# Attention with relative bias and a feed-forward layer on one core: a one-element memset ahead of the last four loads of v

## The chip, the core and the metric

The kernel runs on one core of a Trainium2 chip. The metric is the device time of one execution in microseconds (us). The engines in the profile are PE (TensorE, matmuls; PEld is its weight loads), DVE (VectorE), ACT (ScalarE), POOL (GpSimd) and SP (SyncE, which here only issues DMAs). DMAs that GpSimd issues are in the queue that the profile calls software_dynamic, those of SyncE in hardware_dynamic; both use the core's 16 DMA engines.

## The reference

Attention over 8 batches, 8 heads, 576 positions and a head width of 64, with a bias that depends on the distance of two positions, and behind it a feed-forward layer over all 8 x 576 = 4608 tokens:

```python
scores = scale * q @ k.transpose(0, 1, 3, 2) + bias      # bias from a table of 32 buckets per head
attn = softmax(scores)
x = (attn @ v).transpose(0, 2, 1, 3).reshape(B * S, H * D)   # 4608 x 512
h = x @ w_in                                              # 512 -> 2048
out = np.maximum(0.01 * h, h) @ w_out                     # 2048 -> 512
```

## The kernel before

Work goes by pairs of heads: pair n = 4 b + p is heads 2p and 2p + 1 of batch b, 32 pairs in all. For one pair:

- VectorE copies q and k of the pair, 96 rows wide, from the batch's tiles qn and kn into one of three buffers pr (`rows`, L440). From pair 9 on a DMA of SyncE turns them into a tile tu (`turn_by_dma`, L445; called "the turn" below), and VectorE or ScalarE copies that to qt and kt (L471, L475).
- PE makes the scores (L497 to L505), ScalarE takes the exponential (L511 to L518), VectorE multiplies with the bias (L531), and PE multiplies with v (`av`, L552 and L567), where a column of ones gives the sum.
- VectorE divides by that sum into one of three tiles opair (`norm`, L579, L580), and a DMA of SyncE transposes opair into xT[p], which holds the tokens of four batches in a ring (`x_dma`, L586; pairs 7 and 31 and the first ones go through PE instead). The names that end in numbers, xT_78 to xT_81, are xT[0] to xT[3].

The feed-forward layer goes by tiles T of 512 tokens. The tile T = 2 begins with the last pair of batch 2 (pair 11), T = 3 with that of batch 3 (pair 15), T = 4 with pair 19, T = 5 with pair 23: PE multiplies with w_in (L619; L676 for the last tiles, with fewer products after the sums of L653), ScalarE applies the leaky maximum (L695), PE multiplies with w_out (L749), and VectorE combines the products in y (L760, L765), whose blocks SyncE stores (L769). Seven products stand for eight, so y's blocks are reused, and a write to one waits for the store of the tile before.

The loads of q, k and v are DMAs of GpSimd, which cast float32 to bfloat16. v of batch b goes into vn[b % 2] and v4[b % 2], six DMAs (L307, L313), and can start when PE has read v of batch b - 2 there. The tiles of q and k are double too (L299, four DMAs for a batch).

All engines run in the order in which the program is written, which a planner sets ahead of time: `Plan` places tasks by estimated costs, due times and a table of shifts. `pool_load` puts the loads into one line on GpSimd; in it stand, for each batch b from 2 on, q and k of b, and then v of b. The planner's list of what the load of v waits for has held, for b > 3, the output transpose of the last pair of batch b - 2 (the `xt` of `plan_loads`), but the list only sets the order and the planned times: the program itself waits only for semaphores of data that an instruction reads or writes.

Of the kernel before, what the change touches and what calls it, by code (L numbers as in the profile page):

```python
# [79 lines left out]
class Plan:  # L80
# [37 lines left out]
    def add(self, engine, cost, after, go, rank, take=(), give=(), tail=0.0, at=None):  # L118
        t = {"engine": engine, "cost": cost, "after": list(after), "go": go, "rank": rank, "n": len(self.tasks),
             "take": list(take), "give": list(give), "tail": tail, "end": at, "start": at}  # L120
        if at is None:
            self.tasks.append(t)
        return t
# [95 lines left out]
def kernel(  # L219
# [10 lines left out]
    nc = tc.nc  # L230

    B, H, S, D = q.shape
# [5 lines left out]
    n_pairs = H // 2  # L238
# [24 lines left out]
    RING = 4  # L263
    RT = RING * S
    xT = [per.tile([P, RT + P - SL], BF16, name=f"xT{p}") for p in range(n_pairs)]
# [29 lines left out]
    def load_qk(b, h0, h1, js=(0, 1)):  # L295
        i = b % NBUF
        for j in js:
            src, dst = ((q, qn[i]), (k, kn[i]))[j]
            nc.gpsimd.dma_start(  # L299
                out=dst[0:RQ, h0:h1, :, :].rearrange("r h c d -> r h (c d)"),  # L300
                in_=src[b, h0:h1, :, :].rearrange("h (r c) d -> r h (c d)", c=NC),
            )

    def load_v_part(b, j):
        i = b % NBUF
        for c in ((0,), (1, 2), (3,))[j]:
            nc.gpsimd.dma_start(  # L307
                out=vn[i][:, c, :, 0:D],
                in_=v[b, :, c * P : (c + 1) * P, :].rearrange("h s d -> s h d"),
            )  # L310
        if j == 2:
            for e in range(2):
                nc.gpsimd.dma_start(  # L313
                    out=v4[i][e * SL : (e + 1) * SL, :, e, 0:D],
                    in_=v[b, e::2, NJ * P : S, :].rearrange("h s d -> s h d"),
                )

    def clear_v(eng, i):
        eng.memset(v4[i], 0.0)
        for e in range(2):  # L320
            eng.memset(v4[i][e * SL : (e + 1) * SL, :, e, D : D + 1], 1.0)
        eng.memset(vn[i][:, :, :, D : D + 1], 1.0)
# [452 lines left out]
    rowt, cut, sct, ext, avt, nrt, nmt, xt, vt = {}, {}, {}, {}, {}, {}, {}, {}, {}  # L775
# [19 lines left out]
    def moves(t, work, lane, lead, least, yields=0.39):  # L795
        t["moves"], t["lane"], t["lead"], t["least"], t["yields"] = work, lane, lead, least, yields
        return t

    def pool_load(key, cost, go, work, after=(), rank=1):
        t = add("POOL", cost, prev + list(after), go, rank)  # L800
        moves(t, work, 0, min(cost + 1.0, 3.2), cost + 2.2, 0.39 if key[0] in ("qk", "v") else 0.2)
        prev[:] = [t]
        L[key] = t
        return t
# [5 lines left out]
    prev.append(clears[0])  # L810
    pool_load(("qk", 0, 2), 1.4, lambda: load_qk(0, 6, H), 2.0, rank=-9)
    pool_load(("v", 0), 5.2, lambda: [load_v_part(0, j) for j in range(3)], 5.5, rank=-8)
    vt[0] = L["v", 0]
    edges = add("POOL", 1.0, list(prev), lambda: [clear_edges(nc.gpsimd, i) for i in range(3)], -7)
    pool_load(("qk", 1, 0), 1.4, lambda: load_qk(1, 0, 4), 2.6, rank=-4)
    pool_load(("w_in", 0), 0.8, lambda: load_w_in(0), WH, rank=-4)
    clears.append(add("POOL", 1.2, list(prev), lambda: clear_v(nc.gpsimd, 1), -3))
    prev.append(clears[1])
    vt[1] = pool_load(("v", 1), 5.2, lambda: [load_v_part(1, j) for j in range(3)], VB, rank=-2)
    pool_load(("qk", 1, 1), 1.4, lambda: load_qk(1, 4, H), 2.7, rank=-1)  # L820
    pool_load(("w_in", 1), 0.8, lambda: load_w_in(1), WH, rank=6)
# [139 lines left out]
    def plan_loads(b):  # L961
        i = n_pairs * (b - 2)
        for hh in range(2):
            ps = [rowt[i + 2 * hh + x][r] for x in range(2) for r in range(2)]
            pool_load(("qk", b, hh), 1.5, lambda hh=hh: load_qk(b, 4 * hh, 4 * hh + 4), 3.0, ps, 10 * i + 500)
        avs = [t for p in range(n_pairs) for t in avt[i + p]]
        if b > 3:
            avs = avs + xt[i + n_pairs - 1]
        vt[b] = pool_load(("v", b), 5.0, lambda: [load_v_part(b, j) for j in range(3)], 5.0, avs, 10 * i + 500)

    oin, ins = {}, {}

# [110 lines left out]
    for n in range(N):  # L1083
        if n >= 2 * n_pairs and n % n_pairs == 0:
            plan_loads(n // n_pairs)
        plan_rows(n)
        if n == 0:
            plan_table()
            clears[1]["after"].append(hk4t[1])
        plan_pair(n)  # L1090
# [47 lines left out]
```

## Time and profile before

| | us |
|---|---|
| median of 3 runs (lowest, highest) | 364.35 (362.64, 365.35) |
| the profiled execution | 364.15 |
| its span, from the first to the last instruction | 362.3 |

The granted clock is 1.000 throughout. The page gives PE as busy for 97% of the span, VectorE 81%, ScalarE 76%, GpSimd 19%. Attention runs to about 262 us, beside the feed-forward tiles that are ready by then; from there on only feed-forward products are left. A row of the timeline gives the start, the length, the engine, the line, the operation and, in brackets, how long the engine stood idle before it and what ended that. A row of the DMA view gives what is moved, how many DMAs began or were being issued in the window, their size and the median time from issue to landing.

### The profile page before, as it was taken

The numbers are of one execution on the slowest core, as the hardware profiler recorded it, in microseconds if no ns is written. First come the engines' busy times: TensorE is split into PE (matmuls) and PEld (weight loads), VectorE is DVE, ScalarE is ACT, GpSimd is POOL, SyncE is SP. The second block draws the span as 40 slices with busy tenths as digits, with TensorE's granted clock in tenths as the row PEclk, the third lists the DMA queues.
The fourth block names the chain that finished last, engine by engine and source line by source line (L and its number), as shares of the span: only waits on it lengthen the run. The fifth ranks groups of instructions, "written<-read, shape, count | busy, mean of one in ns | idle before, by whom it ended". The sixth has DMA issues, their size and how long they took to land.

```text
span 362.3 us, 10124 instructions
## 1 busy us (share of the span) xinstructions
PE 351.4 (97%) x4206; PEld 256.6 (71%) x4206; DVE 292.4 (81%) x703; ACT 275.8 (76%) x365; POOL 70.2 (19%) x107
## 2 busy tenths in 40 slices
PE   8999999999999899999998999999999999999996
PEld 6665457745677365654676777667888888888885
DVE  6978799885799559957679979999986778686594
ACT  6987998689778799799988897897737546756520
POOL 8955132080006200800350050000000000000000
PEclk9999999999999999999999999999999999999999
DMA  8999999999539993997499799312120020020022
GB/s 126 151 187 196 208 184 146 132 140 194 130 81 101 202 155 58 133 170 87 59 172 173 103 148 116 97 34 52 51 76 2 31 88 31 2 87 31 31 87 89
DMA packets 106941, 39.31 MB, mean 108 GB/s; under 512 B 82320, under 2 KB 105872, under 8 KB 106896
## 3 DMA queue, kind: packets, MB, share of 16 engines
q0 software_dynamic: 53424, 18.21, 50.0%
q1 hardware_dynamic: 53120, 20.03, 31.6%
q8 instruction: 33, 0.54, 0.6%
q10 hardware_dynamic: 352, 0.43, 0.4%
q14 instruction: 12, 0.10, 0.1%
HBM read 36.70 MB, written 9.44 MB: 127 GB/s over the span
## 4 chain that ended last, share of the span: by engine, by line
PE 52%; DMA 5%; DVE 5%; ACT 5%; issue 2%; DVEq 0%; ACTq 0%
PE pm L749 20%; PE pm L676 12%; PE pm L619 9%; PE ps_s L497 4%; DMA xT<-opair 3%; PE ps_o L567 2%; PE ps_om L567 2%; ACT at L511 2%; DMA out_dram<-y 2%; ACT gt L695 2%; DVE sum L717 1%; DVE y L765 1%; PE ps_s L501 1%; PE ps_s L504 1%; DVE opair L580 1%
## 5 line engine op out<-in xcount | busy, mean ns | idle before, releaser
L511 ACT ACTIVATE at<-ps_s 128x1024 bf16<-128x1024 f32 x124 | 121.3, 1041 | 19.6 <-PE ps_s L497 17.1
L619 PE MATMUL pm<-xT,w_in_sb 128*128 128x512 bf16 (+1 forms) x416 | 86.4, 346 | 3.7 <-DMA xT<-opair 1.6
L531 DVE TENSOR_TENSOR at<-at,hk 128x768 bf16<-128x768 bf16 (+4 forms) x156 | 66.5, 449 | 18.1 <-ACT at L511 14.0
L619 PEld LDWEIGHTS <-w_in_sb 128*128 128x128 bf16 x416 | 37.6, 98 | 35.5 <-issue 9.2
L749 PEld LDWEIGHTS <-gt 128*128 128x128 bf16 x576 | 54.2, 98 | 11.8 <-issue 3.4
L695 ACT ACTIVATE gt<-pm 128x512 bf16<-128x512 f32 x88 | 51.0, 643 | 12.7 <-PE pm L619 12.4
L307 POOL DMA_DIRECT2D vn<-in_v_dram x32 | 28.9, 915 | 133.2 <-PE ps_o L567 70.8
L765 DVE TENSOR_TENSOR y<-pm,y 128x512 f32<-128x512 f32 (+1 forms) x53 | 41.0, 774 | 13.5 <-PE pm L749 13.2
L749 PEld LDWEIGHTS <-sum 128*128 128x128 bf16 x432 | 40.9, 98 | 7.9 <-issue 2.1
L567 PEld LDWEIGHTS <-at 128*128 128x128 bf16 x1240 | 41.6, 98 | 3.4 <-issue 0.9
L497 PE MATMUL ps_s<-qt,kt 64*128 64x512 bf16 x256 | 39.9, 381 | 0.6 <-ACT at L513 0.3
L749 PE MATMUL pm<-w_out_sb,gt 128*128 128x256 bf16 x288 | 37.1, 273 | 0.0
L749 PE MATMUL pm<-mix,gt 128*128 128x256 bf16 x288 | 36.6, 273 | 0.0
L749 PE MATMUL pm<-w_out_sb,sum 128*128 128x256 bf16 x288 | 35.7, 273 | 0.0
L567 PE MATMUL ps_o<-vn,at 128*128 128x65 bf16 x640 | 25.5, 193 | 0.6 <-DMA vn<-in_v_dram 0.5
L680 ACT COPY at<-pm 128x1024 f32<-128x1024 f32 x15 | 15.1, 1008 | 12.5 <-PE pm L676 12.5
L686 DVE TENSOR_TENSOR at<-pm,at 128x512 f32<-128x512 f32 (+1 forms) x22 | 19.0, 879 | 6.8 <-ACT at L680 4.6
L567 PE MATMUL ps_om<-vn,at 128*128 128x65 bf16 x600 | 23.9, 194 | 0.0
L518 ACT ACTIVATE at<-ps_s 128x576 bf16<-128x576 f32 x31 | 21.1, 681 | 2.6 <-PE ps_s L505 2.6
L497 PEld LDWEIGHTS <-kt 64*128 64x128 bf16 x256 | 8.3, 94 | 17.2 <-issue 16.0
L513 ACT ACTIVATE at<-ps_s 128x512 bf16<-128x512 f32 x31 | 19.2, 620 | 0.8 <-PE ps_s L501 0.3
L692 ACT ACTIVATE gt<-at 128x1024 bf16<-128x1024 f32 x15 | 15.8, 1056 | 5.2 <-DVE at L686 5.2
(120 smaller groups left out, 528.3 us busy)
## 6 DMA issues: line engine op xcount, KB each, us to landing
out_dram<-y SPq DMA_DIRECT2D x35, 256.0 KB, 2.2
vn<-in_v_dram POOLq DMA_DIRECT2D x32, 128.0 KB, 6.4
qn<-in_q_dram POOLq DMA_DIRECT2D x14, 288.0 KB, 10.5
kn<-in_k_dram POOLq DMA_DIRECT2D x14, 288.0 KB, 11.3
w_in_sb<-in_moe_w_in_dram POOLq DMA_DIRECT2D x2, 1024.0 KB, 11.2
w_out_sb<-in_moe_w_out_dram POOLq DMA_DIRECT2D x2, 1024.0 KB, 17.4
qn<-in_q_dram POOLq DMA_DIRECT2D x4, 144.0 KB, 4.2
v<-in_v_dram POOLq DMA_DIRECT2D x16, 32.0 KB, 6.8
```

Of the source, the lines that this page charges most:

```text
L307: nc.gpsimd.dma_start(out=vn[i][:, c, :, 0:D], in_=v[b, :, c * P : (c + 1) * P, :].rearrange("h s d -> s h d"),)
L497: nc.tensor.matmul(ps[:, e, :], lhsT=kt[r, u * P : (u + 1) * P], rhs=qt[r, 0:512], start=True, stop=True)
L511: nc.scalar.activation(at[:, :, u, 0:512], ps, AF.Exp, scale=scale)
L513: nc.scalar.activation(at[:, :, :, 512:S].rearrange("p e c i -> p c e i"), ps[:, 0, :].rearrange("p (c e i) -> p c e i", e=2, i=SL), AF.Ex ...
L518: nc.scalar.activation(at4[:, 0:S], ps.rearrange("p e i -> p (e i)")[:, 0:S], AF.Exp, scale=scale)
L531: nc.vector.tensor_tensor(out=o, in0=o, in1=m, op=ALU.mult)
L567: nc.tensor.matmul(ps[:, ic, :], lhsT=at[:, o : o + P], rhs=vn[i][:, c, 2 * p + e, :], start=whole and c == 0, stop=not whole and ic == NJ ...
L619: nc.tensor.matmul(pms[T, f][:, o : o + n], lhsT=w_in_sb[:, c, f * P : (f + 1) * P], rhs=xT[c][:, x : x + n], start=(c == 0 and i == 0), s ...
L676: nc.tensor.matmul(ps[:, i, :], lhsT=w, rhs=x, start=fresh and i % 2 == 0 and c == 0, stop=i % 2 == 1 and c == 1, skip_group_check=not fresh)
L695: nc.scalar.activation(gts[T][:, f, :], pms.pop((T, f)), AF.Prelu, bias=0.0, scale=1.0, alpha=0.01)
L749: nc.tensor.matmul(ps[:, ts, :], lhsT=l[:, ts * P : (ts + 1) * P], rhs=r, start=(ts == 0 or apart) and j == 0, stop=(ts == 1 or apart) and ...
L765: nc.vector.tensor_tensor(out=out_, in0=ps, in1=x, op=ALU.add)
```

## The change

A memset of one element on GpSimd is put ahead of the load of v for the batches 4 to 7. The element lies in xT[3], in the first column behind the 576 tokens of batch b - 2. The transpose of that batch's last pair writes 640 columns, 64 of them into the space behind its tokens, so the memset writes where that DMA has written, and waits for its landing.

```diff
+    def behind_x(b):
+        o = (b - 2) % RING * S + S
+        nc.gpsimd.memset(xT[n_pairs - 1][0:1, o : o + 1], 0.0)
...
-        vt[b] = pool_load(("v", b), 5.0, lambda: [load_v_part(b, j) for j in range(3)], 5.0, avs, 10 * i + 500)
+        vt[b] = pool_load(("v", b), 5.0, lambda: [behind_x(b) if b > 3 else None, [load_v_part(b, j) for j in range(3)]], 5.0, avs, 10 * i + 500)
```

On GpSimd, the place of the load of v for batch 5 (vn_96 and v_1_98 are the second buffers, qn_91 and kn_93 the first ones, for batch 6; what an instruction waits for stands in brackets, DMASW and DMAHW being landings of GpSimd's and SyncE's DMAs). Before:

```order
L307 DMA vn_96<-in_v_dram 128x8x64 [waits DMASW5_49,PE_49]
L307 DMA vn_96<-in_v_dram 128x8x64 [waits DMASW6_49,PE_49]
L307 DMA vn_96<-in_v_dram 128x8x64 [waits DMASW7_49,PE_49]
L307 DMA vn_96<-in_v_dram 128x8x64 [waits DMASW0_49,PE_49]
L313 DMA v_1_98<-in_v_dram 64x4x64 [waits DMASW1_49]
L313 DMA v_1_98<-in_v_dram 64x4x64 [waits DMASW2_49]
L299 DMA qn_91<-in_q_dram 96x4x384 [waits DMASW3_49,DVE_49]
L299 DMA kn_93<-in_k_dram 96x4x384 [waits DMASW4_49,DVE_49]
```

Now:

```order
L320 MEMSET xT_81 1x1 [waits DMAHW0_49]
L307 DMA vn_96<-in_v_dram 128x8x64 [waits DMASW5_49,PE_49]
L307 DMA vn_96<-in_v_dram 128x8x64 [waits DMASW6_49,PE_49]
L307 DMA vn_96<-in_v_dram 128x8x64 [waits DMASW7_49,PE_49]
L307 DMA vn_96<-in_v_dram 128x8x64 [waits DMASW0_49,PE_49]
L313 DMA v_1_98<-in_v_dram 64x4x64 [waits DMASW1_49]
L313 DMA v_1_98<-in_v_dram 64x4x64 [waits DMASW2_49]
L299 DMA qn_91<-in_q_dram 96x4x384 [waits DMASW3_49,DVE_49]
```

Nothing else moves on GpSimd: the memset is new, with a wait for one DMA of SyncE, and the loads behind it stand as they stood.

On SyncE, the transpose that the memset waits for at this place (xT_81 of pair 15) and what follows it. Before:

```order
L445 DMA_TRANSPOSE tu_108<-pr_105 128x12x96 [waits DMAHW0_49,DMAHW7_49,DVE_49,Activation_49]
L586 DMA_TRANSPOSE xT_81<-opair 128x5x128 [waits DVE_49]
L769 DMA out_dram<-y 128x2x256 [waits DMAHW1_49,DVE_49]
L445 DMA_TRANSPOSE tu_109<-pr_106 128x12x96 [waits DMAHW2_49,DVE_49]
L586 DMA_TRANSPOSE xT_78<-opair 128x5x128 [waits DMAHW3_49,DVE_49,PE_49]
```

Now (the line numbers behind the new function are higher by four):

```order
L449 DMA_TRANSPOSE tu_108<-pr_105 128x12x96 [waits DMAHW0_49,DMAHW7_49,DVE_49,Activation_49]
L590 DMA_TRANSPOSE xT_81<-opair 128x5x128 [waits DVE_49,Pool_49]
L773 DMA out_dram<-y 128x2x256 [waits DMAHW1_49,DVE_49]
L449 DMA_TRANSPOSE tu_109<-pr_106 128x12x96 [waits DMAHW2_49,DVE_49]
L590 DMA_TRANSPOSE xT_78<-opair 128x5x128 [waits DMAHW3_49,DVE_49,PE_49]
```

The order is the same; the transpose now also waits for GpSimd, namely for the memset of the batch before, which wrote into the column where this one begins. The transposes of pairs 23 and 27 have got the same wait. PE, VectorE and ScalarE run the same instructions in the same order.

## The prediction

> **What bounds the kernel now.** I read the page first, then the waits, the chain and the timeline around the loads that the change touches.
>
> ```profile
> span 362.3 us, 10124 instructions
> PE 351.4 (97%) x4206; PEld 256.6 (71%) x4206; DVE 292.4 (81%) x703; ACT 275.8 (76%) x365; POOL 70.2 (19%) x107
> ```
>
> PE is busy for 351.4 of 362.3 us, so the kernel is near the bound of its matmul stream, and a change that removes no matmul can win only what PE stands idle, and of that only what a DMA causes. The waits between 105 and 262 us, the stretch from the first changed load to the end of attention, say how much that is:
>
> ```profile
> DVE y L760 <- DMA out_dram<-y: 1.7, 1, 1.7
> PE pm L619 <- DMA xT<-opair: 1.6, 2, 1.3
> PE pm L619 <- DVE opair L580: 1.4, 1, 1.4
> ```
>
> Each row is who waited, for whom, total us, times, longest. The chain of work that ended last runs through the same places:
>
> ```profile
> 113.57 6.30 DMA xT<-opair
> ...
> 147.36 6.04 DMA xT<-opair
> ...
> 182.21 6.25 DMA out_dram<-y
> ...
> 195.92 0.50 DVE opair L580
> ```
>
> Three transfers of about 6 us stand on it (start, length, what). The timeline gives the idle time behind them, in brackets:
>
> ```profile
> 119.91 1.24 PE L619 MATMUL pm<-xT,w_in_sb 128*128 128x512 bf16 x5 [1.26 <-DMA xT<-opair]
> 153.44 0.81 PE L619 MATMUL pm<-xT,w_in_sb 128*128 128x512 bf16 x3 [0.32 <-DMA xT<-opair]
> 188.55 0.69 DVE L760 COPY y<-pm 128x512 f32<-128x512 f32 x1 [1.67 <-DMA out_dram<-y]
> 196.47 0.70 PE L619 MATMUL pm<-xT,w_in_sb 128*128 128x256 bf16 x5 [1.36 <-DVE opair L580]
> ```
>
> PE stands 1.26 us because the last transpose of batch 2 is late, 0.32 us because that of batch 3 is, and 1.36 us because VectorE is late. VectorE was held for 1.67 us at 188.55 by an output store, and from there the chain is VectorE's own work to 196.42. Everything else on PE in this stretch is in step.
>
> **What stands beside these transfers.** The four loads of v that the change moves:
>
> ```profile
> 111.59 3.53 POOL L307 DMA_DIRECT2D vn<-in_v_dram  x4 [31.54 <-PE ps_o L567]
> 145.39 3.52 POOL L307 DMA_DIRECT2D vn<-in_v_dram  x4 [25.80 <-PE ps_om L567]
> 177.91 3.57 POOL L307 DMA_DIRECT2D vn<-in_v_dram  x4 [24.78 <-PE ps_o L567]
> 210.51 3.63 POOL L307 DMA_DIRECT2D vn<-in_v_dram  x4 [24.48 <-PE ps_om L567]
> ```
>
> The first two transposes of a last pair stand in the chain above, the other two in SyncE's timeline, with what it issues next at the third:
>
> ```profile
> 178.55 1.21 SPq L586 DMA_TRANSPOSE xT<-opair  x1
> 180.22 1.52 SPq L445 DMA_TRANSPOSE tu<-pr  x1
> 182.21 0.89 SPq L769 DMA_DIRECT2D out_dram<-y  x1
> ...
> 212.78 1.21 SPq L586 DMA_TRANSPOSE xT<-opair  x1
> ```
>
> Each load starts 0.6 to 2.3 us before its transpose. Now what a transfer of SyncE takes from issue to landing, in windows of the DMA view that hold one of its kind. Alone (issued at 102.74, 201.02 and 223.10):
>
> ```profile
> xT<-opair SPq DMA_TRANSPOSE x1, 2.6
> tu<-pr SPq DMA_TRANSPOSE x1, 3.3
> out_dram<-y SPq DMA_DIRECT2D x1, 256.0 KB, 2.2
> ```
>
> Beside a load of v (issued at 178.55 and 212.78, a turn of q and k at 180.22, and a store at 114.90; 6.30, 6.04 and, for the store at 182.21, 6.25 stand in the chain):
>
> ```profile
> xT<-opair SPq DMA_TRANSPOSE x1, 5.5
> xT<-opair SPq DMA_TRANSPOSE x1, 6.7
> tu<-pr SPq DMA_TRANSPOSE x1, 7.5
> out_dram<-y SPq DMA_DIRECT2D x1, 256.0 KB, 7.2
> ```
>
> So a load stretches a transpose by 2.9 to 4.1 us, and a store by 4 to 5.
>
> **The change, part by part.** *The memset.* The trace has no 1x1 memset; the nearest are these, and one much larger:
>
> ```profile
> L1122 POOL MEMSET const-bfloat16-1.0<- 128x1 bf16 x1 | 0.1, 106 | 0.0
> L319 POOL MEMSET v<- 128x520 bf16 x2 | 1.3, 653 | 0.0
> ```
>
> I bound it by 0 and 0.65 us, and take 0.1 (mean ns is the second number): the 128x1 form is the nearest. Four of them on an engine that is busy for 19% of the span cost nothing by themselves; what counts is the wait. SyncE's three later transposes into the same tile wait for a memset that is over some 30 us earlier: nothing.
>
> *The wait, and what queues behind it.* GpSimd runs in order, so the six DMAs of v and, at the first three places, the four loads of q and k of the next batch start later. By how much: from the old start of the load to the transpose's issue (1.98, 1.97, 0.64, 2.27 us), plus its landing (2.6 alone; 3.3 if another transfer of SyncE is ahead), plus 0.1. That is **4.7 to 5.4, 4.7 to 5.4, 3.3 to 4.0 and 5.0 to 5.7 us**. v itself has cover: the last one's last piece, issued at 214.75, lands near 221.5, with the wait near 227, and its first pair reads it only at
>
> ```profile
> v<-in_v_dram POOLq DMA_DIRECT2D x1, 32.0 KB, 6.7
> ...
> 246.06 0.79 PE L567 MATMUL ps_om<-vn,at 128*128 128x65 bf16 x20
> ```
>
> *The transposes.* With no load ahead, that of batch 2 lands at 113.57 + 2.6 to 3.3 = 116.2 to 116.9. PE comes to its data at 118.65, so the **1.26 us** go, with 1.7 us to spare. That of batch 3 lands at about 150.3; PE comes at 153.12, and the **0.32 us** go. At the third and fourth place PE does not wait for the transpose now, so nothing is won by it directly.
>
> *The store at 182.21.* Here the wait acts on a transfer that it does not name. The third transpose lands at 178.55 + 2.6 = 181.15 and the load is issued near 181.3. Its packets flow later still: in the DMA view of 111.59 to 113.4, behind the first load's issue, there is no row for the software queue at all, and of 145.4 to 147.1 there is
>
> ```profile
> q0 software_dynamic: 15, 0.00, 1.7%
> ```
>
> that is, packets begin about 1.7 us after the issue, here near 183.0. The turn at 180.22 needs 3.3 us alone and is then 0.5 us from its end, and the store, 2.2 us alone, follows it: about 184.4 without sharing, and about 186 if the shared part is stretched two and a half times, as 6.3 to 2.6 was. VectorE comes to L760 at 188.55 − 1.67 = 186.88. So the 1.67 us go, and PE's **1.36 us** with them. I take all of it; both ends are 0 and 1.36.
>
> The Trainium skill, "DMA: Bandwidth & Descriptors", section "Queues, rings and completion order", says that each DMA engine goes round-robin between the queues that have work, a packet at a time. The stretch of 2.1 to 2.6 times above agrees with one rival queue; by it alone a store that shares all its time takes twice its 2.2 us and lands near 186.6, just ahead of L760; at the stretch measured it would land near 187.9 and keep half of its stall, and the sum would be 0.7 us smaller.
>
> *What is late next.* SyncE's transfers behind the load are now met by the loads of q and k, which hurt more. Issued at 118.06 and 152.86, the turns of pairs 18 and 22 took
>
> ```profile
> tu<-pr SPq DMA_TRANSPOSE x1, 13.4
> tu<-pr SPq DMA_TRANSPOSE x1, 12.1
> ```
>
> and landed at 131.5 and 165.0, the former with the last of k, issued at 118.92:
>
> ```profile
> kn<-in_k_dram POOLq DMA_DIRECT2D x1, 288.0 KB, 12.5
> ```
>
> The turn frees a pr buffer, into which VectorE copies three pairs later, in order, for pairs 21 and 26:
>
> ```profile
> 137.53 0.35 DVE L440 COPY pr<-qn 96x768 bf16<-96x768 bf16 x1
> ...
> 173.69 0.35 DVE L440 COPY pr<-qn 96x768 bf16<-96x768 bf16 x1
> ...
> 176.83 0.23 DVE L475 TENSOR_TENSOR qt<-qt,own 128x128 bf16<-128x128 bf16 x1 [1.50 <-ACT qt L471]
> ```
>
> Pair 21 needs the turn of pair 18: 6.0 us of slack now, 4.8 once all runs 1.26 us earlier. If the whole tail of the loads moves by 5.4 us, VectorE stands 0.6 us. Pair 26 needs the turn of pair 23 (issued at 159.27, landing 8.8 us later at 168.0): 5.6 us, less the 1.58 won by then, 4.1, so 1.3 us late at worst, and there 1.50 us of idle VectorE, in the last row, stand behind it. But the tail moves by less than the load does: the transposes and the stores that shared with it are then out of the way, and the turn of pair 18 falls beside v, not beside q and k. I cost this at nothing, 0 to 1.9 us. The copies out of the turns have over 10 us everywhere.
>
> **The sum.** 1.26 + 0.32 + 1.36 = 2.94 us. The profiled execution took 364.15 us, 1.85 more than its span; 364.15 − 2.94 = 361.2. The median of the runs shown is 364.35, which would give 361.4. I say **361.3**, 0.8% less.
>
> **The rivals.** *Only the transposes gain.* If the store still lands after 187, the 1.36 us stay: 364.2 − 1.6 = 362.6. For it: the turn at 180.22 stands ahead of it and five transfers shared that time. Against: the packets start near 183.0. Chance 0.15.
>
> *The gain is eaten.* The late turns cost 1.9 us and the store keeps half of its stall, 0.7 us: 364.2 − 2.9 + 2.6 = 363.9. For it: the work of the loads stays the same, and something of SyncE's always stands beside them. Against: what stands there later has more slack. Chance 0.12. That section of the Trainium skill speaks for this rival too: under round-robin a wait moves the stretch from one transfer to the next.
>
> *Slower, by VectorE's order.* Place: the copy for pair 21 at 137.53. VectorE is without a gap there from 135.3 to 143.9, so each us that it waits for the turn of pair 18 goes to the end. It decides from a shift of the turn of 4.8 us on, and beats the gain from 4.8 + 2.9 = 7.7 us on. That needs the turn to be stretched by v and by q and k in full, one after the other: twice the load's delay, 10.8 us, gives 6.0 us of standstill, 364.2 − 2.9 + 6.0 = 367.3. For it: transfers of 13.4 us exist. Against: in the same trace two stores passed v in 7.2 us each. Chance 0.08.
>
> *The wait does nothing,* since the planner's place of the load, or another wait, already held it: 364.2. Against: the load starts 2 us before the transpose is even issued. Chance 0.05.
>
> *More than the gaps.* On the chain stand 6.30, 6.04 and 6.25 us, and alone they would be 2.6, 2.6 and 2.2, 11.2 us less. PE's ends are modelled, and some standstill may hide in its busy time: 1.5 us more would give 359.7. Chance 0.12.
>
> **How the numbers follow.** The forecast, all three gaps gone, has 0.48. About 1% (3.6 us) is what a measurement of this kernel can tell from no change. The forecast lies at 0.8%, and scatter may carry it over: faster by over 1% gets 0.1 from it and 0.12 from the last rival; slower by over 1% half of the slower one and a little, 0.05; the rest, 0.73, is within 1%. The range runs from 359.6 (nearly all of the last rival) to 365.0 (the eaten gain and no change with their scatter), and leaves out the slower case and a little below.
>
> **What would show it.** The four transposes should land in 2.6 to 3.3 us, each load of v start right behind, and PE's rows at the starts of the two tiles carry no idle time for DMA. L760 should show none for out_dram. Wrong would be: idle time on VectorE's L440 for a turn, a store of over 5 us before L760, or a transpose as long as before, which would mean that the load of v was not what stretched it.

## The result, and the profile after

| | before | after |
|---|---|---|
| median (lowest, highest), 11 runs each, us | 364.85 (362.64, 366.83) | 361.29 (358.99, 365.18) |
| the profiled execution, us | 364.15 | 359.80 |
| its span, us | 362.3 | 358.0 |

The ratio is 0.9888, with an interval of 0.9852 to 0.9923: 1.1% less, and 0.8 to 1.5% is possible. (Ratios here are of undisturbed runs alone, so they are not exactly those of the medians.) The granted clock was 0.998, and 1.00 as far as 353 us, where PE is nearly through. The head of the page:

```profile
span 358.0 us, 10132 instructions
PE 350.8 (98%) x4206; PEld 256.7 (72%) x4206; DVE 292.4 (82%) x703; ACT 275.6 (77%) x365; POOL 71.2 (20%) x111
```

PE does the same 4206 matmuls in nearly the same busy time (350.8 us, 351.4 before), in a span that is 4.3 us shorter. The timeline of GpSimd shows the memset and the load of v at each of the four places:

```profile
115.17 0.09 POOL L320 MEMSET xT<- 1x1 bf16 x1 [36.14 <-DMA xT<-opair]
115.67 3.63 POOL L307 DMA_DIRECT2D vn<-in_v_dram  x4 [0.41 <-issue]
...
147.59 0.09 POOL L320 MEMSET xT<- 1x1 bf16 x1 [24.26 <-DMA xT<-opair]
148.10 4.34 POOL L307 DMA_DIRECT2D vn<-in_v_dram  x4 [0.41 <-PE pm L753]
...
178.32 0.09 POOL L320 MEMSET xT<- 1x1 bf16 x1 [21.91 <-DMA xT<-opair]
178.85 3.91 POOL L307 DMA_DIRECT2D vn<-in_v_dram  x4 [0.43 <-PE ps_s L509]
...
211.22 0.09 POOL L320 MEMSET xT<- 1x1 bf16 x1 [22.31 <-DMA xT<-opair]
211.72 3.94 POOL L307 DMA_DIRECT2D vn<-in_v_dram  x4 [0.41 <-PE ps_s L501]
```

Each memset is released by the transpose, and the load follows 0.50 to 0.53 us behind the memset's start. In the DMA view, around the issue of each of the four transposes (112.54, 144.96, 175.63 and 208.61) and of the store that VectorE had waited for (now issued at 179.29), the landing times are

```profile
xT<-opair SPq DMA_TRANSPOSE x1, 2.6
...
out_dram<-y SPq DMA_DIRECT2D x1, 256.0 KB, 2.8
```

All four transposes give the first row, against 6.3, 6.0, 5.5 and 6.7 us before, and the store took 2.8 instead of 6.25. Between 105 and 262 us the waits have one row with a DMA in it, GpSimd's own; those of PE and VectorE that the prediction quoted are gone:

```profile
POOL xT L320 <- DMA xT<-opair: 104.6, 4, 36.1
...
POOL kn L299 <- DVE sum L721: 2.2, 1, 2.2
...
PE pm L623 <- ACT gt L699: 0.2, 1, 0.2
```

**Where the time came from.** PE runs the same instructions in both traces, so the start of one before, minus the start of the same one after, says how much had been won by then. PE's timeline of before, in pairs of rows ahead of and behind each of the three gaps, and one further on:

```profile
117.19 0.38 PE L501 MATMUL ps_s<-qt,kt 128*128 128x128 bf16 x4
121.08 0.60 PE L497 MATMUL ps_s<-qt,kt 64*128 64x512 bf16 x4
...
152.08 0.39 PE L501 MATMUL ps_s<-qt,kt 128*128 128x128 bf16 x4
154.18 0.61 PE L497 MATMUL ps_s<-qt,kt 64*128 64x512 bf16 x4
...
190.41 0.61 PE L497 MATMUL ps_s<-qt,kt 64*128 64x512 bf16 x4
197.34 0.38 PE L504 MATMUL ps_s<-qt,kt 128*128 128x512 bf16 x1
202.21 0.39 PE L501 MATMUL ps_s<-qt,kt 128*128 128x128 bf16 x4
```

and the same instructions after:

```profile
116.16 0.38 PE L505 MATMUL ps_s<-qt,kt 128*128 128x128 bf16 x4
118.64 0.60 PE L501 MATMUL ps_s<-qt,kt 64*128 64x512 bf16 x4
...
149.64 0.39 PE L505 MATMUL ps_s<-qt,kt 128*128 128x128 bf16 x4
151.25 0.61 PE L501 MATMUL ps_s<-qt,kt 64*128 64x512 bf16 x4
...
187.49 0.61 PE L501 MATMUL ps_s<-qt,kt 64*128 64x512 bf16 x4
192.89 0.38 PE L508 MATMUL ps_s<-qt,kt 128*128 128x512 bf16 x1
197.94 0.38 PE L505 MATMUL ps_s<-qt,kt 128*128 128x128 bf16 x4
```

The differences are 1.03, 2.44, 2.44, 2.93, 2.92, 4.45 and 4.27 us. So 1.03 us lay ahead of the first changed load and is scatter between two profiles: a second profile of the changed kernel has −0.07 there (table below). Behind it come three steps, at the three gaps that the prediction named: **+1.41, +0.49 and +1.53**, then −0.18, and nothing to the end. The change is worth 4.27 − 1.03 = **3.24 us** of this trace, 0.9%.

### The profile page after: what moved, and what is told of

It is laid out like the page before. It is cut to its first block, busy times and chain, and to the rows that moved or that the text cites. A ratio compares the mean times of both kernels' runs of the same rounds, so it can differ in the third digit from the quotient of the medians.

```text
span 358.0 us, 10132 instructions
## 1 busy us (share of the span) xinstructions
PE 350.8 (98%) x4206; PEld 256.7 (72%) x4206; DVE 292.4 (82%) x703; ACT 275.6 (77%) x365; POOL 71.2 (20%) x111
## 4 chain that ended last, share of the span: by engine, by line
PE 78%; DMA 8%; POOL 4%; DVE 3%; ACT 3%; issue 2%; POOLq 0%; DVEq 0%; ACTq 0%
PE pm L753 30%; PE pm L623 16%; PE pm L680 12%; PE ps_s L501 7%; DMA w_out_sb<-in_moe_w_out_dram 5%; PE ps_om L571 4%; PE ps_o L571 4%; DMA vn<-in_v_dram 3%; PE ps_s L505 2%; POOL vn L307 1%; PE ps_s L508 1%; ACT at L515 1%; DVE sum L721 1%; ACT gt L699 1%; PE ps_o L556 1%
## 5 line engine op out<-in xcount | busy, mean ns | idle before, releaser
L769 DVE TENSOR_TENSOR y<-pm,y 128x512 f32<-128x512 f32 (+1 forms) x53 | 41.1, 775 | 13.4 <-PE pm L753 13.2
L307 POOL DMA_DIRECT2D vn<-in_v_dram x32 | 30.4, 963 | 26.8 <-PE ps_o L571 13.2
## 6 DMA issues: line engine op xcount, KB each, us to landing
kn<-in_k_dram POOLq DMA_DIRECT2D x14, 288.0 KB, 12.2
```

Source lines behind the costliest of these rows:

```text
L307: nc.gpsimd.dma_start(out=vn[i][:, c, :, 0:D], in_=v[b, :, c * P : (c + 1) * P, :].rearrange("h s d -> s h d"),)
L769: nc.vector.tensor_tensor(out=out_, in0=ps, in1=x, op=ALU.add)
```

## The experiments

For each run, that difference was taken at stations between the places, and the steps are given in the table. "Lead at 105" is what the run was ahead (or, below zero, behind) before the first changed load: scatter, except in the last three rows, whose kernels change something ahead of it. The third step holds the −0.18. Every ratio is against runs of the kernel before in the same series; the steps all use the one profile of before.

| run | median us (before) | ratio, interval | lead at 105 | steps at places 1, 2, 3, 4 |
|---|---|---|---|---|
| changed kernel | 361.29 (364.85) | 0.9888, 0.9852 to 0.9923 | 1.03 | 1.42, 0.48, 1.34, 0.00 |
| place 1 alone | 363.15 (364.94) | 0.9937, 0.9909 to 0.9964 | −0.46 | 1.40, 0.12, −0.34, 0.00 |
| place 2 alone | 364.45 (364.94) | 0.9966, 0.9933 to 0.9999 | 0.00 | 0.12, 0.46, −0.43, −0.01 |
| place 3 alone | 361.87 (364.94) | 0.9921, 0.9894 to 0.9949 | 0.80 | −0.28, 0.23, 1.34, −0.01 |
| place 4 alone | 364.69 (364.94) | 0.9999, 0.9972 to 1.0026 | 0.70 | −0.17, 0.15, −0.34, −0.28 |
| v early, q and k wait | 365.49 (364.52) | 1.0018, 0.9981 to 1.0054 | −0.42 | −0.30, 0.35, −1.98, −0.01 |
| a wait a pair longer | 364.28 (364.52) | 0.9960, 0.9917 to 1.0002 | −4.58 | 1.30, 0.48, 1.34, −0.82 |
| these loads left out | 361.69 (364.52) | 0.9899, 0.9862 to 0.9936 | −1.59 | 1.42, 0.48, 1.33, −0.01 |
| without place 4 | 361.14 (364.52) | 0.9916, 0.9877 to 0.9956 | −2.25 | 1.42, 0.47, 1.34, 0.00 |
| changed kernel again | 361.00 (365.27) | 0.9906, 0.9872 to 0.9940 | −0.07 | 1.42, 0.49, 1.34, −0.01 |
| and batch 3 waits | 361.08 (365.27) | 0.9907, 0.9871 to 0.9943 | 0.04 | 1.42, 0.47, 1.35, −0.22 |
| its second half waits | 359.64 (365.27) | 0.9863, 0.9828 to 0.9898 | 2.16 | 1.40, 0.47, 1.35, −0.21 |
| each half waits | 359.87 (365.27) | 0.9870, 0.9835 to 0.9905 | 2.05 | 1.43, 0.46, 1.35, −0.21 |

### One place at a time

The memset ahead of the load for one batch alone; the other three kernels have 5, 6 and 7 for the 4:

```diff
-        vt[b] = pool_load(("v", b), 5.0, lambda: [behind_x(b) if b > 3 else None, ...
+        vt[b] = pool_load(("v", b), 5.0, lambda: [behind_x(b) if b == 4 else None, ...
```

> The memset stands only ahead of the load for batch 4 (first place). Sharing theory (a load of v stretches whatever SyncE has under way, and only the late transfers that PE or VectorE wait for cost time): the transpose of pair 11 lands in 2.6 to 3.3 us, PE's idle time before the first products of tile 2 is gone and PE is then 1.3 to 1.5 us earlier than in the kernel before; the idle times at tile 3 (0.32) and of VectorE for the store (1.67), with PE's 1.36, stay. In all 1.3 to 1.5 us less, about 363.4. Rival (a general relief of the DMA engines, the same at each of the four places): about 0.8 us less, and not at tile 2 alone. Rival (most of the difference between the two profiles lies ahead of the change): nothing that PE's start times show after 119 us.

> The memset stands only ahead of the load for batch 5 (second place). Sharing theory: the transpose of pair 15 lands in 2.6 to 3.3 us, PE's 0.32 us of idle time at tile 3 are gone and PE gains 0.3 to 0.5 us there, nothing elsewhere: about 364.4. General relief: about 0.8 us less.

> The memset stands only ahead of the load for batch 6 (third place). Sharing theory: the store that VectorE waits for lands in 2.2 to 3.5 us, VectorE's 1.67 us of idle time ahead of the copy to y and PE's 1.36 us behind it are gone, and PE gains 1.4 to 1.5 us there, nothing elsewhere; the transpose of pair 19 that the memset waits for is not waited for by PE. About 363.4. General relief: about 0.8 us less. If only the transposes mattered: nothing.

> The memset stands only ahead of the load for batch 7 (fourth place). Sharing theory: the transpose of pair 23 lands in 2.6 us instead of 6.7, and nobody waits for it: no change of PE's start times beyond 0.2 us, about 364.8. General relief: about 0.8 us less.

Each of the first three takes its own step and leaves the others within scatter of 0.1 to 0.4 us. With place 3 alone, PE's timeline still has the first gap and not the third; with place 1 alone it is the other way:

```profile
119.39 1.24 PE L623 MATMUL pm<-xT,w_in_sb 128*128 128x512 bf16 x5 [1.54 <-DMA xT<-opair]
```

```profile
195.74 1.03 PE L623 MATMUL pm<-xT,w_in_sb 128*128 128x256 bf16 x8 [1.69 <-DVE opair L584]
```

The steps of the three add up: 1.40 + 0.46 + 1.34 = 3.20, against 3.24 together. The gaps that stay in these runs are 1.14 to 1.54 and 1.69 long where before had 1.26 and 1.36: that is the scatter in the columns of places 1 and 3. The −0.28 at place 4 in the last of the four, like the −0.2 in the last three rows of the table, is not explained. In the timed runs the four give 0.63 + 0.34 + 0.79 + 0.01 = 1.8%, more than the 1.1% of the whole; the intervals, each some 0.3 to either side, allow both. For place 3 the timed 0.5 to 1.1% lies above the 1.3 us (0.4%) of its trace; what makes that difference stays open.

### Is it v that stretches the transfers, or the loads at large?

Here v is loaded early, as before, and the memset stands ahead of the q and k that come behind it:

```diff
-            pool_load(("qk", b, hh), 1.5, lambda hh=hh: load_qk(b, 4 * hh, 4 * hh + 4), 3.0, ps, 10 * i + 500)
+            pool_load(("qk", b, hh), 1.5, lambda hh=hh: [behind_x(b - 1) if hh == 0 and b > 4 else None, load_qk(b, 4 * hh, 4 * hh + 4)], ...
-        ... lambda: [behind_x(b) if b > 3 else None, [load_v_part(b, j) for j in range(3)]], 5.0, avs, 10 * i + 500)
+        ... lambda: [load_v_part(b, j) for j in range(3)], 5.0, avs, 10 * i + 500)
```

> The loads of v start as in the kernel before; the memset stands behind them, ahead of the loads of q and k of the next batch (three places). Sharing theory (it is v's packets that stand beside the transpose of the last pair and the store): the transposes still take over 5 us, the idle times at tile 2, at tile 3 and at the store stay within 0.4 us, and the time is that of the kernel before within 1 us. Rival (q and k are what hurts, since the turns beside them take 12 to 13 us): the gain of the whole change, 3 us.

Neither of the two large steps is won: the transposes took 6.6, 5.6 and 5.5 us, against 6.3, 6.0 and 5.5 before. The second place shows 0.35 us, where its transpose took 0.4 us less; in the three runs above that change nothing there it shows 0.12 to 0.23. The chain of work that ended last has the first transpose and the store on it, as before:

```profile
114.00 6.60 DMA xT<-opair
...
182.57 8.24 DMA out_dram<-y
```

and VectorE's timeline shows what the store then costs:

```profile
190.91 0.69 DVE L764 COPY y<-pm 128x512 f32<-128x512 f32 x1 [3.66 <-PE pm L623]
```

The row names PE, but the store lands at 182.57 + 8.24 = 190.81, just ahead of this copy's start: it is the store that ends the 3.66 us. With q and k out of the way the transposes are nearly as slow as ever, so it is v's packets that stretch them. They stretch the store as well: from 182.57 to 190.81 the DMA view counts 256 packets between 512 B and 2 KB, just the store's own of 1 KB, so those of q and k, of 768 B, had not begun when it landed. That the store was 2 us slower than before, so that VectorE stood 3.66 us instead of 1.67, was not expected, and its cause stays open.

### Does a longer wait cost what the slower rival said?

The memset waits for the transpose of the next batch's first pair instead (pairs 12, 16, 20, 24), and the program issues the loads only behind that transpose (by a list `held_back`, which is not shown), so that they start later still, at 127.87, 162.20, 192.97 and 224.50:

```diff
     def behind_x(b):
-        o = (b - 2) % RING * S + S
-        nc.gpsimd.memset(xT[n_pairs - 1][0:1, o : o + 1], 0.0)
+        o = (b - 1) % RING * S + S
+        nc.gpsimd.memset(xT[0][0:1, o : o + 1], 0.0)
```

> The memset waits for the transpose of the next batch's first pair (pairs 12, 16, 20, 24), so the four loads of v, and q and k behind them, start some 6 to 7 us later still than in the changed kernel; the order of every other engine is the same. The rival of the prediction that ends slower says when lateness costs: VectorE copies q and k out of the loaded tiles in its order. In the changed kernel the least slack between a landing and such a copy is 5.6 us at pair 20, 5.0 at pair 24, 2.6 at pair 26 (for a turn) and 1.0 at pair 28. With 6 to 7 us more: VectorE stands 0 to 1 us at pair 20, 1 to 3 us at pairs 24 to 26 and 4 to 6 us at pair 28, and the kernel is 3 to 8 us slower than the changed one, that is level with the kernel before or up to 4 us slower. If lateness is covered (turns and transposes land earlier when loads come later): within 1 us of the changed kernel.

Now VectorE does stand at its copies of q and k, as that rival had it, though mostly for the loads themselves and hardly for a turn. The waits between 105 and 262 us:

```profile
DVE pr L452 <- DMA kn<-in_k_dram: 4.4, 4, 1.4
...
DVE pr L452 <- DMA qn<-in_q_dram: 0.8, 1, 0.8
...
PE pm L634 <- DVE opair L592: 0.6, 1, 0.6
DVE pr L452 <- DMA tu<-pr: 0.5, 1, 0.5
```

That is 5.7 us of standstill, and of it 0.82 us reach PE (the fourth step) and perhaps 0.12 more (the first). The rest does not reach PE. The price that I gave such standstill was too high by a factor of six over all, but not everywhere: 1.40 us of the first row stand ahead of the copy at 206.09, and PE's loss follows at once, behind VectorE's next opair:

```profile
207.53 0.60 PE L634 MATMUL pm<-xT,w_in_sb 128*128 128x256 bf16 x4 [0.64 <-DVE opair L592]
```

In the timed runs the ratio, 0.9960, lies 1.6 us above the 0.9916 of the kernel without place 4 (same series), with intervals of some 1.5 us to either side, and the medians lie 3.1 us apart; this trace shows no more than 0.9 us of that. That the span of this profile is 364.6 us has its cause ahead of 105 us, below.

### How much is there to win from these loads at all?

This kernel leaves out v of batches 4 to 7 and q and k of 5 to 7, and the memsets with them:

```diff
+            ... load_qk(b, 4 * hh, 4 * hh + 4) if b < 5 else None, ...
+        ... [load_v_part(b, j) for j in range(3 if b < 4 else 0)], 5.0, avs, 10 * i + 500)
```

> The loads of v for batches 4 to 7 and of q and k for batches 5 to 7 are left out (those batches compute on what the buffers hold), and so is the memset. This bounds what these loads still cost in the changed kernel. Sharing theory, with PE's idle time as the whole price: PE is no earlier than in the changed kernel by more than 0.3 us at any place after 119 us, and the time is that of the changed kernel within 0.5 us. Rival (some standstill hides in PE's modelled busy time): 1.5 us or more below the changed kernel.

The steps are those of the changed kernel to 0.01 us, the −0.18 among them. So the change wins all that these loads cost PE, and the −0.18 isn't theirs; what makes it I have not found. The next kernel takes the fourth place away (`behind_x(b) if 3 < b < 7 else None`):

> The memset at the first three places only. Sharing theory: the whole gain, as the fourth place gains nothing; PE's start times after 220 us are within 0.2 us of the changed kernel's. If each place had a share: 0.8 us less gain.

The steps are the same again: the fourth memset does nothing here.

### The same cure at another place

The two profiles that are furthest behind at 105 us, with −4.58 and −2.25, lost 3.5 and 3.0 us of that between 60 and 105 us, nearly all of it from 73 to 77 us. In the kernel before, SyncE's turn of pair 10, issued at 59.39, meets the loads of q and k of batch 3; ScalarE waits for it and PE for ScalarE. DMA view, ScalarE's and PE's timeline of before:

```profile
tu<-pr SPq DMA_TRANSPOSE x1, 11.5
...
70.96 1.19 ACT L471 COPY qt<-tu 128x576 bf16<-128x576 bf16 x1 [2.02 <-DMA tu<-pr]
...
73.12 0.38 PE L501 MATMUL ps_s<-qt,kt 128*128 128x128 bf16 x4 [1.17 <-ACT at L511]
```

The same in the run with the longer wait, which is where it lost its 3.5 us:

```profile
tu<-pr SPq DMA_TRANSPOSE x1, 13.7
...
74.19 1.17 ACT L483 COPY qt<-tu 128x576 bf16<-128x576 bf16 x1 [4.17 <-DMA tu<-pr]
...
76.33 0.38 PE L513 MATMUL ps_s<-qt,kt 128*128 128x128 bf16 x4 [3.11 <-ACT at L523]
```

The longer standstill, 3.11 us against 1.17, is 1.9 of the 3.5 us. Another 1.4 us are lost in the matmuls just behind it, which run at half the granted clock (a row gives the stretch, its length, PE's busy time and matmuls, the granted clock, the DMA share and GB/s):

```profile
78.00:80.00 2.00, 2.00 (x11) 0.50 3.87 138
```

In the kernel before, behind its 1.17 us, the clock stays at 1.00. The run without place 4 shows the same pair: 3.25 us of standstill, and a granted clock of 0.50 from 74 to 76 us.

So I put a copy of one element out of that turn's tile on GpSimd, ahead of all four loads of q and k of batch 3, ahead of the second two alone, or ahead of the second two with another copy, out of pair 9's turn, ahead of the first two. Behind the helper, the three kernels differ in one table: `{0: 10}`, `{1: 10}` and `{0: 9, 1: 10}`:

```diff
+    seen = per.tile([P, 1], BF16, name="seen")
...
+                nc.gpsimd.tensor_copy(out=seen[0:1, 0:1], in_=tu_[m % NTU][0:1, 0, 0:1])
...
-            ... lambda hh=hh: load_qk(b, 4 * hh, 4 * hh + 4), 3.0, ps, 10 * i + 500)
+            ... lambda hh=hh: behind_turn({1: 10}.get(hh, 0) if b == 3 else 0, lambda: load_qk(b, 4 * hh, 4 * hh + 4)), ...
```

> The changed kernel again, as measure for the three beside it and for the scatter ahead of the change. Sharing theory: PE gains 1.4, 0.5 and 1.5 us at tile 2, tile 3 and behind the store, whatever the profile shows ahead of 100 us; the time is 0.7 to 1.5% below the kernel before.

> The changed kernel, and in addition a one-element copy on GpSimd that reads the turn of pair 10 stands ahead of the four loads of q and k for batch 3. Now these are issued near 53 to 57 us and the turns of pairs 9 and 10 beside them take 10 to 16 us; ScalarE waits 1.9 to 4.2 us for the turn of pair 10 near 70 us and PE stands 1.0 to 3.3 us behind that. Sharing theory: without the loads beside it the turn lands near 63 to 66 us, ScalarE's wait and PE's standstill near 72 us go: 1 to 3 us less than the changed kernel. Its danger is lateness: the loads start near 64 us, land near 70 to 76 us and VectorE wants the first of them at 68 to 70 us; if that decides, VectorE stands 2 to 4 us and the kernel is not faster, or up to 3 us slower, than the changed one.

> As the run before, but only the second half of q and k for batch 3 (heads 4 to 7) waits for the turn of pair 10; the first half starts as it does now. Sharing theory: the turn of pair 10 lands by 66 us instead of 70 to 74, ScalarE's wait for it and PE's standstill near 72 us go, and the second half, wanted at 75 us, is not late: 1 to 3 us less than the changed kernel. If the first half and v alone stretch the turns as much: no change.

> As the run before, and in addition the first half waits for the turn of pair 9. Sharing theory: the turn of pair 9 lands near 60 us instead of 64 to 72, which nobody waits for by more than 1 us, so about the time of the run before, or worse if the first half comes late to VectorE's copy at 68 us.

With all four loads held, the turn takes 3.3 us and PE is 1.3 us earlier at the old gap, but now k is late, and 0.5 us are lost again just behind it; 0.6 us more go near 82 us, behind a wait of VectorE for a later turn (1.99 us). VectorE's and PE's timeline of that run:

```profile
70.13 0.36 DVE L462 COPY pr<-kn 96x768 bf16<-96x768 bf16 x1 [0.66 <-DMA kn<-in_k_dram]
...
73.93 0.45 PE L617 MATMUL ps_tx<-ident,opair 128*128 128x128 bf16 x5 [0.43 <-DVE opair L603]
```

Its time, 361.08, is that of the changed kernel, 361.00. With the second half held alone, the copy on GpSimd and the turn are

```profile
65.15 0.56 POOL L335 COPY seen<-tu 1x1 bf16<-1x1 bf16 x1 [9.38 <-DMA tu<-pr]
...
tu<-pr SPq DMA_TRANSPOSE x1, 6.2
```

and neither ScalarE nor PE waits for the turn any more. Its median is 359.64 us (358.90 to 360.57, 6 runs); seven of the eight runs of the changed kernel in that series (359.52 to 362.67) lie above its highest. It is the **fastest version**: 0.9863 of the kernel before, with 0.9828 to 0.9898. Holding both halves, each for its own turn, gives the same within scatter, 359.87.

## Why the prediction was right

The forecast, 361.3 us, met the median, 361.29, by all three gaps that it summed; that it meets it to 0.01 is luck, with scatter of 2 us to either side. The forecast took 3.05 us off a median of 364.35; the runs took 3.56 off one of 364.85. Its steps in turn:

- **The terms.** 1.26, 0.32 and 1.36 were the gaps of the timeline; the steps were 1.42, 0.48 and 1.53, each larger by 0.16 to 0.17. Such a gap is read from a matmul's modelled end, and it is too short by that much here. Less the 0.18 that comes back, 3.24 against a sum of 2.94.
- **The load's delay.** With the lead of each place taken off, the loads start 5.11, 5.16, 3.86 and 5.48 us later (at place 1, 115.67 + 1.03 − 111.59 = 5.11). The forecasts were 4.7 to 5.4, 4.7 to 5.4, 3.3 to 4.0 and 5.0 to 5.7. They hold although the 0.41 to 0.44 us from the memset's end to the load's issue were left out: the transposes landed at the lower end, 2.6.
- **The store** was the boldest step, and it held: predicted landing 184.4 to 186 (with a stretch of two and a half its own figures give 186.5, still ahead of VectorE's 186.88), measured 179.29 + 2.75 = 182.04, which by the old clock, 2.92 later, is 184.96. VectorE's copy L764 starts at 183.87 with no idle time in its row. What carries it is the late start of v's packets; of the window from 178.85, the load's issue, to 181.3 the DMA view says

```profile
q0 software_dynamic: 2, 0.00, 0.2%
```

 so they begin 2.4 us behind the issue, not the 1.7 that I took, and v's packets are hardly beside the store at all.
- **What is late next.** "The tail moves by less than the load does" was **wrong**. The last k of the first place, now issued at 122.66, takes the 12.2 us of the row below and lands at 134.86 + 2.45 = 137.31 by the old clock, 5.9 us later than its 131.44, where the load moved by 5.1; at the next two places it is 6.1 and 7.4 us where the load moved by 5.2 and 3.9. The second half of that sentence was right: the turn of pair 18 falls beside v and took 6.7 us instead of 13.4. But the next one, of pair 19, now falls beside q and k and took 12.0 instead of 9.1. The DMA view at the issue of these three:

```profile
tu<-pr SPq DMA_TRANSPOSE x1, 6.7
...
kn<-in_k_dram POOLq DMA_DIRECT2D x1, 288.0 KB, 12.2
...
tu<-pr SPq DMA_TRANSPOSE x1, 12.0
```

 No copy into pr waits for either, so the cost was the nothing that I had put down.
- **The round-robin rule** of the Trainium skill, "DMA: Bandwidth & Descriptors", "Queues, rings and completion order", spoke for a stretch that only moves on. It does move on, as the two rows of turns show; 6.7 is twice the 3.3 of a turn alone, what two queues in turns would give if their packets took equally long, and 12.0 is far more, so the trace agrees with the rule in direction, and equal turns do not give the size. At the store of the changed kernel it could not be weighed, since hardly any packet of v flowed beside it. My "2.1 to 2.6 times" took in only the transposes and the turn: in the kernel before, the stores, 6.25 and 7.2 us against 2.2, were stretched 2.8 and 3.3 times.
- **The rivals.** *Only the transposes gain* falls with the third step. *The gain is eaten* falls, for the late turns had their slack. *Slower, by VectorE's order* was right about the place and the kind of wait and wrong on the price: "each us that it waits for the turn goes to the end" was shown to be untrue by the longer wait: there VectorE stood 0.79 and 1.05 us right ahead of that very copy, at 141.03 and 142.44, and PE lost at most 0.12. VectorE has no gap there, but PE was not waiting for it. *The wait does nothing* falls with the memset's rows. *More than the gaps* holds for 0.5 of its 1.5 us, the 0.16 to 0.17 in each step; beyond that it falls, since leaving the loads out wins no more. That the profiled execution came out at 359.80, near its 359.7, is the 1.03 us from ahead of the change.

## What to carry to other kernels

Two queues that share the DMA engines can be ordered by data: a one-element write or read on the engine that issues the bulk load, in a tile that the urgent transfer writes, holds the load until that transfer has landed, for 0.1 to 0.6 us of an engine that is idle. It pays where somebody waits for the urgent transfer and nobody for the load, and only for as much as the load can be late: half a load held back won 1.4 us where the whole one held back won nothing. Look also for the transfer that the wait doesn't name but that is issued right behind it; here it gave nearly half of the gain.

## What the runs showed of the hardware

- Packets of GpSimd's loads of v began 1.6 to 2.4 us behind the issue (the first by 149.70 for the load of 148.10, by 181.3 for that of 178.85), and a store that SyncE issued 0.44 us behind such a load passed nearly undisturbed (2.75 us, against 2.2 alone).
- A turn that is 3.3 us alone took 10.7 to 13.7 us at one place, that of pair 10, in the eleven profiles in which nothing held the loads of q and k beside it, and PE stood 0.3 to 3.25 us behind it. A stretch of transfers that share the engines is thus not only long but uneven, and where PE waits at its end, it can spread the times: in one series the kernel before ranged over 362.5 to 369.0 us (13 runs), the changed one over 359.5 to 362.7 (8), and the fastest one over 358.9 to 360.6 (6). That the turn makes this spread was not shown.
- In the two profiles in which PE stood over 3 us there, the granted clock fell to 0.50 for some 3.4 us (77.7 to 81.1 in one, 73.8 to 77.2 in the other), which cost another 0.9 to 1.4 us; behind standstills of up to 1.8 us at the same place it stayed at 1.00. A late transfer can thus cost more than the time that PE waits for it.
